# Masks put into the score banks a segment ahead, denominators behind the V products, LayerNorm steps behind the out-projection

## The chip, the cores and the metric

The kernel runs on one core of a Trainium2 chip. Five engines work beside each other, each through its own list of instructions in order: TensorE (PE, with its weight loads shown as PEld), VectorE (DVE), ScalarE (ACT), GpSimd (POOL) and SyncE (SP, which here only starts transfers). They wait for each other by semaphores. TensorE writes into PSUM, eight banks of 128 partitions by 2 KB; VectorE and ScalarE read PSUM and write the large memory SBUF. The metric is the device time of one execution in microseconds.

## The reference

The reference computes a forward pass and all its gradients. The change concerns the forward pass of the first block, a transformer with a recurrent memory of 8 rows that goes through the sequence in 64 segments of 32 rows:

```python
n_seg = S // seg_len                      # 2048 // 32 = 64
mask = (idx[:, None] < M) | (idx[:, None] >= idx[None, :])
mem = mem0
for s in range(n_seg):
    xs = x[:, s * seg_len:(s + 1) * seg_len, :].copy()
    h = jnp.concatenate([mem, xs], axis=1)            # 8 + 32 rows of 512
    q = jnp.einsum('btd,dhe->bhte', h, Wq)            # 32 heads of 128; k, v alike
    scores = jnp.einsum('bhqe,bhke->bhqk', q, k) * scale
    scores = jnp.where(mask[None, None], scores, -1000000000.0)
    p = _softmax(scores, axis=-1)
    o = jnp.einsum('bhqk,bhke->bhqe', p, v)
    o = jnp.einsum('bhte,hed->btd', o, Wo)
    mem = o[:, :M, :].copy()                          # goes into the next segment
    outs.append(o[:, M:, :])
```

x here is a LayerNorm of the input, scaled and shifted by a modulation. A gated MLP follows, and then the gradients by all inputs. Each segment needs the memory rows of the one before, so the 64 segments form one chain.

## The kernel before

The kernel has stages: `phase2` is the forward loop over the 64 segments, `phase3` the MLP, `phase4` and `phase5` the gradients. Only the forward loop and two helpers are touched. In the forward loop every engine's order is the order in which the Python code issues the instructions: a call at the end of the loop (`self.pin(i0)`) ties each instruction to the one before it on its engine. Waits between engines come from a framework that follows which tile, and which PSUM buffer, an instruction reads or writes.

Four segments make a tile of 128 rows; `s4` is the place of a segment in its tile. The 32 heads are held in 11 groups of three heads (a group is 120 rows wide: three heads of 40 rows, of which 8 are memory rows, 24 the first rows of the segment and 8 its last rows), and the 11 groups in three parts (`pi` = 0, 1, 2) of 4, 4 and 3 groups, one PSUM bank for each part.

A segment goes like this. The projections k, q and v multiply the segment's columns `hT` with the weights, in halves (`col_pass`, L249), and DVE and ACT cast each half to rows `RA`. The halves of k and q are turned (`turns`, L258) and copied into the columns `kT` and `qT`. Then:

- `st_exp(pi)` (L686 to L694): for each group of a part a score product and behind it a mask product, which adds the mask by an identity; then ACT's exp of the whole part into `ET`.
- `vshift` (L719 to L726), between the second and the third part: three products shift the rows of the last V heads in a bank (`sh_ps`), and DVE copies that bank into `Vst`.
- `den(pi)` (L698 to L704): sums over the keys, one column for each group, in a bank of their own (`dc_ps`). `recip` (L709) takes their reciprocals to `rden` on DVE.
- `pv(pi)` (L728 to L733): the V products, into `or_ps`.
- `ost(pi)`: `or_ps` times `rden` into `Ost`; parts 0 and 2 by DVE (L745), part 1 by four instructions of ACT (L742).
- `ott(pi)`: `Ost` is transposed (L716) and copied into `OT`, parts 0 and 2 by DVE, part 1 by ACT.
- `outproj` (L752, products at L220): the out-projection, 64 products into `at_ps`. `split_pair` splits it into a high part (ACT, L227) and a low part (DVE, L229), and `sum_pair` (L232) folds both by products (L237) into `at_ft`, whose memory rows ACT copies into the next segment's `hT` (L842).

Into this chain other work is set at fixed places: `fill(s4, ...)` projects and turns, for the next tile, the last 8 rows of each segment, which do not depend on the memory (slots f1, f2 and turn; POOL's tail copies, L65, put them into `kT` and `qT`); `TailRows` projects the outputs of those rows, once a tile, in two pieces; `pop_later` does the transposes that store a segment's output (L330); for s = 8 to 23 `mod_rest` computes parts of the modulation; and `p1` computes the LayerNorm of a tile two tiles ahead, in five steps: 0 loads, 1 takes statistics, 2 scales (L401, L402), 3 shifts and stores (L406, L407), 4 transposes (L412). Step 0 is at the start of s4 = 0; steps 1 to 3 stand between the k and the q projection of s4 = 1 to 3; step 4 stands before `ott(0)` at s4 = 3.

PSUM is divided into seven buffers that all these tiles share, and one for `TailRows`.

Of the kernel before, what the change touches and what calls it, by code (L numbers as in the profile page):

```python
# [40 lines left out]
class K:  # L41
# [389 lines left out]
    def phase2(self):  # L431
# [13 lines left out]
        with ExitStack() as ctx:  # L445
            wp = ctx.enter_context(tc.tile_pool(name="p2w", bufs=1))
            Wo = wp.tile([128, H, D], BF16, name="Wo")
            maskT = wp.tile([128, 120], BF16, name="maskT128")
# [51 lines left out]
            with tc.tile_pool(name="p0", bufs=1) as p0:  # L500
# [7 lines left out]
                nc.tensor.matmul(m_ps[:], lhsT=perm[:], rhs=mcol[:], start=True, stop=True)  # L508
                nc.vector.tensor_copy(maskT[0:120, :], m_ps[:])
                p1(0, 0)  # L510
# [88 lines left out]
            def b_pieces(t):  # L599
# [10 lines left out]
                def turn_b(x):  # L610
                    bt[x] = btp.tile([128, 8, 128], BF16, name="b_cols" + x)
                    tps = [turn_half(RBt[x], hf) for hf in range(2)]

                    def f():
                        for hf in range(2):
                            self.evac(("act", "dve")[hf], bt[x][:, 4 * hf:4 * hf + 4, :], tps[hf][:])

                    evacs.append(f)
# [23 lines left out]
            mod_r = []  # L642
            tail = TailRows(self, sb2, psp, psb, 1, "ao", self.AOB, 2)

# [10 lines left out]

            i0 = len(self.traced())
            for s in range(NS):
                s4 = s % nseg_t
# [27 lines left out]
                def st_exp(pi):  # L686
                    st_ps = ps_f32("st_ps")
                    for j in range(min(PG, G - pi * PG)):
                        g = pi * PG + j
                        nc.tensor.matmul(st_ps[:, j, 0:120], lhsT=x120(KT, g), rhs=QT[:, g * 120:g * 120 + 120],  # L690
                                         start=True, stop=False)
                        nc.tensor.matmul(st_ps[:, j, 0:120], lhsT=self.ident[:, :], rhs=maskT[:, :], start=False, stop=True)
                    n = min(PG, G - pi * PG)
                    nc.scalar.activation(part3(ET, pi)[:, 0:n, 0:120], st_ps[:, 0:n, 0:120], AF.Exp, scale=cfg.scale)  # L694

                den_ps = [None]

                def den(pi):  # L698
                    if pi == 0:
                        den_ps[0] = psp.tile([128, G], F32, name="dc_ps", tag="p")  # L700
                    n = min(PG, G - pi * PG)
                    for j in range(n):
                        g = pi * PG + j
                        nc.tensor.matmul(den_ps[0][:, g:g + 1], lhsT=ET[:, g * GW:(g + 1) * GW], rhs=self.ones[:, 0:1],  # L704
                                         start=True, stop=True)

                def recip(a, b):
                    a, b = a * PG, min(b * PG, G)
                    nc.vector.reciprocal(rden[:, a:b], den_ps[0][0:120, a:b])  # L709

# [8 lines left out]
                def vshift():  # L719
                    sh = ps_f32("sh_ps")  # L720
                    shf = sh[:].rearrange("p g x -> p (g x)")
                    for hl in range(3):
                        nc.tensor.matmul(shf[32 * hl:32 * hl + 32, 0:384], lhsT=self.ident[96:128, 96:128],
                                         rhs=RA["v"][96:128, 384 * hl:384 * hl + 384], start=True, stop=True,
                                         tile_position=(96, 32 * hl))
                    nc.vector.tensor_copy(Vst[0:96, 1024:1408], shf[0:96, 0:384])  # L726

                def pv(pi):  # L728
# [62 lines left out]
                st_exp(1)  # L791
                vshift()
# [39 lines left out]
                if s + 1 < NS:  # L832
                    tails_in("kq", s + 1)
# [1042 lines left out]
class TailRows:  # L1876

    def __init__(self, k, pool, psp, psb, n, name, dram_b, npieces=4, tags=""):  # L1880
        self.k, self.pool, self.psp, self.psb, self.n, self.name = k, pool, psp, psb, n, name
        self.dram_b, self.npieces, self.tags = dram_b, npieces, tags
        self.cur = None
        self.pieces = []
        self.whole = None
# [10 lines left out]
    def begin(self, s0, ws):  # L1896
# [8 lines left out]
        def piece(u):  # L1905
            def f():
                if u == 0:
                    st["ps"] = self.psb.tile([128, 512], F32, name=f"{self.name}_tps", tag="b")
# [118 lines left out]
```

## Time and profile before

| what | value |
|---|---|
| median of 6 runs | 3183.32 us (3179.41 to 3192.8) |
| profiled execution | 3192.96 us, span 3191.1 us, mean granted clock 0.983 |
| busy over the span | PE 2980.8, PEld 1728.6, DVE 1588.4, ACT 1159.7, POOL 1475.8 us |
| forward loop, 50 to 1010 us | PE 926.65, PEld 598.05, DVE 595.52, ACT 468.75, POOL 626.99 us busy of 960 |
| transfers in that stretch | DMA engines busy 0.84, 203 GB/s |

A line of the timeline gives the start in us from the beginning of the span, the length (of several equal instructions together where it ends in x and a number), the engine, the line of the kernel, the operation, what it writes and reads, the sizes, and in brackets how long the engine had been idle before it and whose work ended that. TensorE's products are pipelined: a row of 0.22 us does not keep the next from starting 0.05 us later, so busy time on PE also counts products that are only draining. A line on a tile gives the shortest, median and longest duration in ns.

### The profile page before, as it was taken

Reading aid. Unit: us, or ns where it says so; the run is one execution under the profiler, and the core shown is the slowest. Engines: PE = TensorE matmul, PEld = TensorE weight load, DVE = VectorE, ACT = ScalarE, POOL = GpSimd, SP = SyncE. Lnnn points to the kernel's source line nnn. Section 1 sums busy time; section 2 is a strip of 40 time slices with the busy share of each in tenths; the row PEclk is TensorE's granted clock in tenths of the full one; section 3 lists DMA queues with packets and bytes.
Section 4 is the critical chain, followed back from the end, with each engine's and each line's share of the span. In section 5 each row is a group of like instructions: output and inputs, shape, how many; then the busy total and the mean of one; then the engine's idle time right before and its main releaser. Section 6 shows DMA issues by size and latency. Waiting matters only on the chain.

```text
span 3191.1 us, 98793 instructions
## 1 busy us (share of the span) xinstructions
PE 2980.8 (93%) x39993; PEld 1728.6 (54%) x40069; DVE 1588.4 (50%) x3770; ACT 1159.7 (36%) x2829; POOL 1475.8 (46%) x2973
## 2 busy tenths in 40 slices
PE   5999999999998899989999999999999969999999
PEld 3666666666665444445555555555555534445454
DVE  4666666665655777642255444555545521332221
ACT  2454444444444333322244444444444410010011
POOL 3666666666664566521244444444444421232322
PEclk8999999999999899999999999999999989999999
DMA  9788888788888799897599999999999999998885
GB/s 300 199 213 202 203 204 203 204 201 212 198 200 244 175 221 215 218 281 242 176 262 256 255 245 257 263 266 259 274 267 258 258 224 227 226 218 190 205 228 154
DMA packets 958892, 726.12 MB, mean 228 GB/s; under 512 B 656018, under 2 KB 831138, under 8 KB 958308
## 3 DMA queue, kind: packets, MB, share of 16 engines
q1 hardware_dynamic: 827940, 508.77, 70.7%
q0 software_dynamic: 59056, 148.62, 13.8%
q10 hardware_dynamic: 71440, 62.40, 7.8%
q8 instruction: 316, 5.18, 0.7%
q14 instruction: 140, 1.15, 0.1%
HBM read 294.91 MB, written 276.33 MB: 179 GB/s over the span
## 4 chain that ended last, share of the span: by engine, by line
PE 30%; DMA 11%; issue 10%; POOL 3%; ACT 2%; DVE 1%; SPq 1%; ACTq 0%; POOLq 0%; DVEq 0%
PE dh_ps L212 9%; PE pass_ps L249 4%; PE g_ps L1509 3%; PE gps L1820 3%; PE dh_tps L212 2%; DMA rows<-OSR 2%; DMA rows<-DKR 2%; PE tps L1424 2%; DMA dOst<-RBd 1%; PE dp_ps L1488 1%; PE dp_ps L1496 1%; ACT RAd L61 1%; DMA rows<-DQR 1%; DMA out_dram<-ot 1%; DMA Kst<-KST 1%
## 5 line engine op out<-in xcount | busy, mean ns | idle before, releaser
L1820 PE MATMUL gps<-rows,hrows 128*128 128x512 bf16 (+2 forms) x2124 | 417.4, 356 | 6.7 <-DVE ot L63 2.8
L1820 PEld LDWEIGHTS <-hrows 128*128 128x128 bf16 x2160 | 211.8, 98 | 210.7 <-issue 7.4
L249 PEld LDWEIGHTS <-hT 128*32 128x32 bf16 x6144 | 158.0, 97 | 161.2 <-issue 1.6
L1538 POOL COPY dOst<-RAd 96x512 bf16<-96x512 bf16 x128 | 78.1, 610 | 355.8 <-DVE RAd L63 345.2
L852 POOL TENSOR_TENSOR Pst<-Pst,rden 120x1408 bf16<-120x1408 bf16 x63 | 160.4, 2546 | 111.7 <-issue 77.8
L1824 POOL DMA_DIRECT2D out_dram<-ot x108 | 81.3, 753 | 238.1 <-DVE ot L63 140.2
L63 DVE CAST ot<-gps 128x512 bf16<-128x512 f32 (+3 forms) x76 | 47.9, 632 | 254.8 <-PE gps L1820 133.1
L309 DVE TENSOR_TENSOR dh_lo<-dh_ps,dh_hi 128x256 bf16<-128x256 f32 x128 | 48.4, 420 | 241.5 <-ACT dh_hi L305 241.5
L1833 PE MATMUL gps5o<-WoT,rows 128*128 128x512 bf16 x588 | 132.4, 384 | 25.2 <-DMA rows<-OSR 24.4
L61 ACT ACTIVATE ot<-gps 128x512 bf16<-128x512 f32 (+3 forms) x75 | 41.1, 548 | 288.0 <-PE gps L1820 138.6
L212 PE MATMUL dh_ps<-WvT,dVT 128*32 128x512 bf16 x2048 | 135.0, 381 | 0.0
L1498 DVE SCALAR_TENSOR_TENSOR dS<-dp_ps,Pst_l 128x512 bf16<-128x512 f32 (+1 forms) x192 | 112.2, 640 | 42.5 <-PE dp_ps L1496 42.4
L249 PE MATMUL pass_ps<-Wv,hT 128*32 128x512 bf16 x2048 | 133.3, 380 | 0.0
L249 PE MATMUL pass_ps<-WoT,dyT 128*32 128x512 bf16 x2048 | 121.9, 380 | 5.2 <-ACT dyT L1597 5.2
L220 PE MATMUL at_ps<-Wo,OT 128*32 128x256 bf16 x4096 | 124.3, 274 | 0.5 <-DVE OT L63 0.2
L61 ACT ACTIVATE dVT<-g_ps 128x512 bf16<-128x512 f32 (+1 forms) x192 | 107.8, 562 | 45.3 <-PE g_ps L1509 27.1
L249 PE MATMUL pass_ps<-Wk,hT 128*32 128x512 bf16 x2048 | 122.7, 382 | 1.5 <-ACT hT L842 1.1
L212 PE MATMUL dh_ps<-WkT,dKT 128*32 128x512 bf16 x2048 | 122.9, 380 | 0.1
L212 PE MATMUL dh_ps<-WqT,dQT 128*32 128x512 bf16 x2048 | 122.4, 379 | 0.0
L249 PE MATMUL pass_ps<-Wq,hT 128*32 128x512 bf16 x2048 | 121.6, 379 | 0.0
L63 DVE CAST RA0v<-pass_ps 128x512 bf16<-128x512 f32 x128 | 88.3, 690 | 65.3 <-PE pass_ps L249 65.1
L694 ACT ACTIVATE ET<-st_ps 128x480 bf16<-128x480 f32 (+1 forms) x192 | 96.0, 535 | 54.2 <-ACT qT L61 37.3
(411 smaller groups left out, 7032.7 us busy)
## 6 DMA issues: line engine op xcount, KB each, us to landing
OSR<-Ost SPq DMA_DIRECT2D x64, 352.0 KB
OT<-OT SPq DMA_DIRECT2D x64, 352.0 KB
VT<-VTr SPq DMA_DIRECT2D x64, 352.0 KB
PS<-Pst SPq DMA_DIRECT2D x64, 352.0 KB
OT_l<-OT SPq DMA_DIRECT2D x64, 352.0 KB
Pst_l<-PS SPq DMA_DIRECT2D x64, 352.0 KB
VT_l<-VT SPq DMA_DIRECT2D x64, 352.0 KB
DKR<-rows_x POOLq DMA_DIRECT2D x64, 352.0 KB, 5.7
```

The costliest lines, as they stand in the source:

```text
L61: return nc.scalar.activation(out, in_, AF.Copy)
L63: return nc.vector.tensor_copy(out, in_)
L212: self.nc.tensor.matmul(ps[32 * j:32 * j + 32, :], lhsT=lhsT, rhs=w, start=(n < 4), stop=(n >= total - 4), tile_position=(0, 32 * j))
L220: nc.tensor.matmul(ps[32 * j:32 * j + 32, :], lhsT=x[k], rhs=w[k][:, 256 * d:256 * d + 256], start=(n == 0), stop=(n == total - 1), tile_p ...
L249: self.nc.tensor.matmul(ps[32 * j:32 * j + 32, :], lhsT=lhs(c), rhs=rhs, start=(c == 0), stop=(c == DC - 1), tile_position=(0, 32 * j))
L694: nc.scalar.activation(part3(ET, pi)[:, 0:n, 0:120], st_ps[:, 0:n, 0:120], AF.Exp, scale=cfg.scale)
L852: nc.gpsimd.tensor_tensor(Pst[0:120, :, :], Pst[0:120, :, :], rden[:, :].unsqueeze(2).to_broadcast([120, G, 128]), op=ALU.mult)
L1498: nc.vector.scalar_tensor_tensor(out=part3(dS, pi), in0=ps[:, 0:n, :], scalar=cfg.scale, in1=part3(Pst, pi), op0=ALU.mult, op1=ALU.mult)
L1509: nc.tensor.matmul(ps[:, j, :], lhsT=lh[:, g * GW:(g + 1) * GW], rhs=rh[:, g * GW:(g + 1) * GW], start=True, stop=True)
L1820: nc.tensor.matmul(ps[:, 0:ng * E], lhsT=hrows[:, tp_, c * 128:(c + 1) * 128], rhs=rows[:, tp_, 0:ng * E], start=(tp_ == 0), stop=(tp_ == ...
L1824: nc.gpsimd.dma_start(outw[c * 128:(c + 1) * 128, h0:h0 + 3 * (ng - 1) + 1:3, :], ot[:, 0:ng * E].rearrange("p (h e) -> p h e", e=E))
L1833: nc.tensor.matmul(pss[gg][:], lhsT=rows[:, tp_, gg * E:(gg + 1) * E], rhs=dyrows[:, tp_, :], start=(tp_ == order[0]), stop=(tp_ == order[ ...
```

## The change

Each of the three score banks is now reserved (a pool `pst` of three banks) and gets its mask by one product over all its groups, `mask_mm`, a segment ahead; the score products add to it. `mask_mm` is called three times before the loop, and in each segment: two times before `ott(0)` where no turn stands there, else one time behind `ott(0)` and one behind `ott(1)`; the last behind `ott(2)`.

The denominators stand behind the V products of their part, and have no bank of their own: parts 0 and 1 are written into columns of the `vshift` bank that the shift does not use, part 2 into free columns of the third `or_ps`. `ott` copies parts 0 and 2 by ACT and part 1 by DVE. `sum_pair` takes all high products first, then the low ones. `turn_b` uses one bank for both halves. The LayerNorm steps 1 to 3 stand behind the out-projection of s4 = 0 to 2, before the tail copies and `split_pair`. The shared buffers are five, and `TailRows` takes its bank from them.

```diff
-        for c in range(self.cfg.DC):
-            for i in range(2):
+        for i in range(2):
+            for c in range(self.cfg.DC):
                 self.nc.tensor.matmul(ft[:, c, :], lhsT=parts[i][:, (c % 2) * 128:(c % 2) * 128 + 128],
-                                      rhs=self.foldhalf[:, c // 2, :], start=(i == 0), stop=(i == 1))
+                                      rhs=self.foldhalf[:, c // 2, :], start=(i == 0 and c == 0), stop=(i == 1),
+                                      skip_group_check=True)
...
-            psp = ctx.enter_context(tc.tile_pool(name="p2ps", bufs=7, space=PSUM))
-            psb = ctx.enter_context(tc.tile_pool(name="p2psb", bufs=1, space=PSUM))
+            psp = ctx.enter_context(tc.tile_pool(name="p2ps", bufs=5, space=PSUM))
+            pst = ctx.enter_context(tc.tile_pool(name="p2pst", bufs=3, space=PSUM))
...
+            def mask_mm(pi):
+
+                n = min(PG, G - pi * PG)
+                ps = masked[pi] = pst.tile([128, PG, GW], F32, name="st_ps", tag="st")
+                nc.tensor.matmul(ps[:, 0:n, 0:120], lhsT=self.ident[:, :], rhs=maskT[:, 0:n, :], start=True, stop=False,
+                                 skip_group_check=True)
...
                 def st_exp(pi):
-                    st_ps = ps_f32("st_ps")
-                    for j in range(min(PG, G - pi * PG)):
-                        g = pi * PG + j
-                        nc.tensor.matmul(st_ps[:, j, 0:120], lhsT=x120(KT, g), rhs=QT[:, g * 120:g * 120 + 120],
-                                         start=True, stop=False)
-                        nc.tensor.matmul(st_ps[:, j, 0:120], lhsT=self.ident[:, :], rhs=maskT[:, :], start=False, stop=True)
+                    st_ps = masked.pop(pi)
...
-                        nc.tensor.matmul(den_ps[0][:, g:g + 1], lhsT=ET[:, g * GW:(g + 1) * GW], rhs=self.ones[:, 0:1],
+                        nc.tensor.matmul(st_ps[:, j, 0:120], lhsT=x120(KT, g), rhs=QT[:, g * 120:g * 120 + 120],
+                                         start=False, stop=True, skip_group_check=True)
...
+                def den(pi, ps):
+                    for g in range(pi * PG, min(pi * PG + PG, G)):
+                        nc.tensor.matmul(ps[:, PG - 1, g:g + 1], lhsT=ET[:, g * GW:(g + 1) * GW], rhs=self.ones[:, 0:1],
                                          start=True, stop=True)
...
-                    self.evac("act" if pi == 1 else "dve", part3(OT, pi)[:, 0:n, :], ps)
+                    self.evac("dve" if pi == 1 else "act", part3(OT, pi)[:, 0:n, :], ps)
...
-                if 1 <= s4 <= 3:
-                    p1(s // nseg_t + P1_AHEAD, s4)
                 proj("q", 0, "dve")
...
-                den(0)
                 or0 = pv(0)
+                den(0, sh)
...
-                den(1)
-                recip(0, 2)
                 or1 = pv(1)
+                den(1, sh)
+                recip(0, 2, sh)
                 ost(0, or0, "dve")
                 ost(1, or1, "act")
-                den(2)
                 or2 = pv(2)
-                recip(2, 3)
+                den(2, or2)
+                recip(2, 3, or2)
                 ost(2, or2, "dve")
+                more = list(range(NP)) if s + 1 < NS else []
+                turned = bool(slots.get((s4, "turn")))
                 fill(s4, "turn")
                 if s4 == 3:
                     p1(s // nseg_t + P1_AHEAD, 4)
+                    turned = True
+                if more and not turned:
+                    mask_mm(more.pop(0))
+                    mask_mm(more.pop(0))
                 ott(0)
+                if len(more) > 1:
+                    mask_mm(more.pop(0))
                 ott(1)
+                if len(more) > 1:
+                    mask_mm(more.pop(0))
                 ott(2)
+                if more:
+                    mask_mm(more.pop(0))
...
                 at_ps = outproj()
                 evac_turned()
+                if s4 < 3:
+                    p1(s // nseg_t + P1_AHEAD, s4 + 1)
```

More of the change, by code (lines that the diff above doesn't have):

```diff
@@ L447, in phase2 @@
             Wo = wp.tile([128, H, D], BF16, name="Wo")
-            maskT = wp.tile([128, 120], BF16, name="maskT128")
+            maskT = wp.tile([128, PG, 120], BF16, name="maskT128")
             nc.vector.memset(maskT[:], NEG)
@@ L508, in phase2 @@
                 nc.tensor.matmul(m_ps[:], lhsT=perm[:], rhs=mcol[:], start=True, stop=True)
[L509 removed]
+                nc.vector.tensor_copy(maskT[0:120, :, :], m_ps[:].unsqueeze(1).to_broadcast([120, PG, 120]))
                 p1(0, 0)
@@ L611, in turn_b @@
                     bt[x] = btp.tile([128, 8, 128], BF16, name="b_cols" + x)
-                    tps = [turn_half(RBt[x], hf) for hf in range(2)]
+                    tp = psp.tile([128, 8, 128], BF16, name="turn_ps", tag="p")
+                    for i in range(8):
+                        nc.tensor.transpose(tp[:, i, :], RBt[x][:, i * 128:(i + 1) * 128], self.ident[:, :])
                     def f():
                         for hf in range(2):
-                            self.evac(("act", "dve")[hf], bt[x][:, 4 * hf:4 * hf + 4, :], tps[hf][:])
+                            self.evac(("act", "dve")[hf], bt[x][:, 4 * hf:4 * hf + 4, :], tp[:, 4 * hf:4 * hf + 4, :])
                     evacs.append(f)
@@ L642, in phase2 @@
             mod_r = []
-            tail = TailRows(self, sb2, psp, psb, 1, "ao", self.AOB, 2)
+            tail = TailRows(self, sb2, psp, psp, 1, "ao", self.AOB, 2, ptag="p")
+            masked = {}
+            def mask_mm(pi):
[3 more added lines that the diff above has]
+                                 skip_group_check=True)
             def tails_in(xs, s):
@@ L656, in phase2 @@
             i0 = len(self.traced())
+            for pi in range(NP):
+                mask_mm(pi)
             for s in range(NS):
@@ L686, in st_exp @@
                 def st_exp(pi):
-                    st_ps = ps_f32("st_ps")
-                    for j in range(min(PG, G - pi * PG)):
-                        g = pi * PG + j
-                        nc.tensor.matmul(st_ps[:, j, 0:120], lhsT=x120(KT, g), rhs=QT[:, g * 120:g * 120 + 120],
-                                         start=True, stop=False)
-                        nc.tensor.matmul(st_ps[:, j, 0:120], lhsT=self.ident[:, :], rhs=maskT[:, :], start=False, stop=True)
[L693 to L700, printed above, removed]
+                    st_ps = masked.pop(pi)
                     n = min(PG, G - pi * PG)
@@ L703, in den, with recip @@
                         g = pi * PG + j
-                        nc.tensor.matmul(den_ps[0][:, g:g + 1], lhsT=ET[:, g * GW:(g + 1) * GW], rhs=self.ones[:, 0:1],
+                        nc.tensor.matmul(st_ps[:, j, 0:120], lhsT=x120(KT, g), rhs=QT[:, g * 120:g * 120 + 120],
+                                         start=False, stop=True, skip_group_check=True)
+                    nc.scalar.activation(part3(ET, pi)[:, 0:n, 0:120], st_ps[:, 0:n, 0:120], AF.Exp, scale=cfg.scale)
+                def den(pi, ps):
+                    for g in range(pi * PG, min(pi * PG + PG, G)):
+                        nc.tensor.matmul(ps[:, PG - 1, g:g + 1], lhsT=ET[:, g * GW:(g + 1) * GW], rhs=self.ones[:, 0:1],
                                          start=True, stop=True)
-                def recip(a, b):
+                def recip(a, b, ps):
                     a, b = a * PG, min(b * PG, G)
-                    nc.vector.reciprocal(rden[:, a:b], den_ps[0][0:120, a:b])
+                    nc.vector.reciprocal(rden[:, a:b], ps[0:120, PG - 1, a:b])
                 def transposes_part(src, pi, w=GW):
@@ L726, in vshift @@
                     nc.vector.tensor_copy(Vst[0:96, 1024:1408], shf[0:96, 0:384])
+                    return sh
                 def pv(pi):
@@ L791, in phase2 @@
                 st_exp(1)
-                vshift()
+                sh = vshift()
                 st_exp(2)
@@ L1876, with __init__ @@
 class TailRows:
-    def __init__(self, k, pool, psp, psb, n, name, dram_b, npieces=4, tags=""):
+    def __init__(self, k, pool, psp, psb, n, name, dram_b, npieces=4, tags="", ptag="b"):
         self.k, self.pool, self.psp, self.psb, self.n, self.name = k, pool, psp, psb, n, name
-        self.dram_b, self.npieces, self.tags = dram_b, npieces, tags
+        self.dram_b, self.npieces, self.tags, self.ptag = dram_b, npieces, tags, ptag
         self.cur = None
@@ L1907, in f @@
                 if u == 0:
-                    st["ps"] = self.psb.tile([128, 512], F32, name=f"{self.name}_tps", tag="b")
+                    st["ps"] = self.psb.tile([128, 512], F32, name=f"{self.name}_tps", tag=self.ptag)
                 for n in range(u * per, (u + 1) * per):
```

## The prediction

> **What bounds the kernel now.** I read four views in this order: the engine table and slices of the page, the busy time of the forward stretch, the timeline of one of its segments engine by engine, and the groups of the tiles that the change moves.
>
> ```profile
> PE 2980.8 (93%) x39993; PEld 1728.6 (54%) x40069; DVE 1588.4 (50%) x3770; ACT 1159.7 (36%) x2829; POOL 1475.8 (46%) x2973
> ...
> 50.00:1010.00 960.00, 926.65 (x17786) 598.05 (x17784) 595.52 (x1479) 468.75 (x1275) 626.99 (x1339) 1.00 0.84 203
> ```
>
> The change lies in the forward loop, the first 1010 us, where PE reads 926.65 of 960 us busy at a granted clock of 1.00. That looks like an engine with nothing to win but instructions. The timeline says otherwise. Segment 33 of the 64, from its first score product at 559.81:
>
> ```profile
> 559.81 0.23 PE L690 MATMUL st_ps<-qT,kT 128*128 128x120 bf16 x1
> ...
> 560.75 0.34 PE L723 MATMUL sh_ps<-RA0v,ident 32*32 32x384 bf16 x3
> 561.35 0.24 PE L704 MATMUL dc_ps<-ones,ET 128*128 128x1 bf16 x4
> 561.45 0.38 PE L733 MATMUL or_ps<-Vst,ET 128*128 128x128 bf16 x4
> 561.67 0.24 PE L704 MATMUL dc_ps<-ones,ET 128*128 128x1 bf16 x4
> 561.77 0.38 PE L733 MATMUL or_ps<-Vst,ET 128*128 128x128 bf16 x4
> 562.21 0.21 PE L704 MATMUL dc_ps<-ones,ET 128*128 128x1 bf16 x3
> 562.32 0.33 PE L733 MATMUL or_ps<-Vst,ET 128*128 128x128 bf16 x3
> 562.94 1.09 PE L716 MATMUL tps<-ident,Ost 128*128 128x128 bf16 x11 [0.29 <-DVE Ost L745]
> 563.87 0.22 PE L330 MATMUL ao_b_tp<-ident,ao_b_tb 128*128 128x128 bf16 x1
> 563.93 0.22 PE L330 MATMUL at_tp<-ident,at_tb 128*128 128x128 bf16 x1
> 564.08 0.40 PE L220 MATMUL at_ps<-Wo,OT 128*32 128x256 bf16 x6
> ```
>
> ```profile
> 560.00 0.69 DVE L63 CAST RA0v<-pass_ps 128x512 bf16<-128x512 f32 x1 [0.31 <-PE pass_ps L249]
> 561.14 0.55 DVE L726 CAST Vst<-sh_ps 96x384 bf16<-96x384 f32 x1 [0.45 <-PE sh_ps L723]
> 561.95 0.21 DVE L709 RECIPROCAL rden<-dc_ps 120x8 f32<-120x8 f32 x1 [0.26 <-PE dc_ps L704]
> 562.19 0.69 DVE L745 TENSOR_TENSOR Ost<-or_ps,rden 120x512 bf16<-120x512 f32 x1
> 562.80 0.17 DVE L709 RECIPROCAL rden<-dc_ps 120x3 f32<-120x3 f32 x1
> 563.08 0.56 DVE L745 TENSOR_TENSOR Ost<-or_ps,rden 120x384 bf16<-120x384 f32 x1
> 563.55 0.88 DVE L63 COPY OT<-tps 128x512 bf16<-128x512 bf16 x2
> ```
>
> From the first score product to the out-projection is 4.27 us here, and the chain is DVE's from 561.95 on: reciprocal, first Ost, second reciprocal, second Ost (ends 563.64), the last transposes behind it, then two small transposes and the projection. PE waits between 562.54 and 562.94 for the first Ost. So a segment's length follows the time of the first reciprocal, 2.14 us after the first score. By place in the tile (s4 = 0, 1, 2, 3) the projection starts 4.41, 4.27, 4.21 and 4.31 us after the first score, nearly the same in every segment; what follows it, up to the next first score, is 10.48 us wherever nothing interferes.
>
> **Part 1: masks.** Removed: 11 mask products at the score products' pitch of 0.052 us, 0.58 us of PE. Added: three products of 480, 480 and 360 columns; no row shows one. At the pitch of the 120-column rows they cost 0.21, 0.21 and 0.16 us, again 0.58; at the worst each stands for the whole 0.39 us of a 512-column pass product. I take the pitch, since four of those pass products, side by side, follow each other every 0.22 us; the other end would add 64 x 0.23 = 15 us for the last mask. Work is moved, not saved. The first exp starts when four scores are done: four fewer products, 0.21 us earlier. But the vshift products (L723) wait for the second RA0v cast (560.69; they start 0.06 later, 560.75), and that does not move: the third score part, behind them, and so the third exp, gains only 0.16 us. Where the masks go: in s4 0 and 1 two stand in the 0.40 us (soon longer) wait before the first transposes, free while that wait exists (without it 0.42 us). The third stands behind the last transposes, which come at the end of DVE's chain, so its 0.16 us lies on the path everywhere. In s4 2 and 3 the masks stand between the transposes.
>
> **Part 2: denominators.** They no longer have a bank; the first two parts write the spare columns of the vshift bank, and in the program the first of them waits for DVE's copy out of that bank (L726). That copy ends at 561.69, so the denominators cannot start before 561.75; before, the first four ran at 561.35, beside the copy. Behind them in PE's order stand the second V products (0.22 us) and the second denominators: 561.75 + 0.10 + 0.22 = 562.07, results 0.24 later, and DVE takes them up 0.04 later (as 561.67 + 0.24 to 561.95): the reciprocal at 562.35 instead of 561.95, **0.40 us late**, though exp was earlier. The wait for the first reciprocal by the third denominators (562.21) is gone; the third part is not late, since DVE reaches its reciprocal only when the first Ost is done. In the 16 segments with modulation products the same order holds and the same 0.40.
>
> **Part 3: which engine copies OT.** OT parts 0 and 2 go to ACT, part 1 to DVE. ACT's four Ost pieces end at 563.47, so 563.87 when late by 0.40; its 0.60 us copy of part 0 then ends about 564.4, before PE gets to the projection, except in s4 3: there ACT has the 0.60 us copy hx (L414, whose next copy starts 0.50 later) in front.
>
> **Sum of parts 1 to 3 per segment.** s4 0 and 1: 0.40 + 0.16 s4 0 and 1: 0.395 + 0.158 = 0.55.. s4 2: the second mask also pushes the last transposes, past their input, by 0.10: 0.64. s4 3: ACT's pieces end 4.06 after the first score, hx starts 0.12 before that, part 0 starts 0.50 later and ends at 5.04, projection at 5.10 instead of 4.31: 0.79. Last tile, no turns: 0.55 for all. 34 x 0.55 + 15 x 0.64 + 15 x 0.79 = **+40 us**.
>
> **Part 4: fold sum.** Four hi products now stand before the lo products, which wait for at_lo 0.21 us after the first hi. Three products at 0.025 us leave the path: 64 x 0.08 = **-5 us**; the copy into hT behind them is covered by the next tile's 1 us of projection (the fill in slot f2), as before.
>
> **Part 5: LayerNorm steps.** Now they stand between the k and q casts on DVE:
>
> ```profile
> L401 DVE TENSOR_SCALAR xh<-x,mv,rstd x14: 540/2318/2869, 80.0 to 870.1; 128x512 f32<-128x512 bf16 x14
> ...
> 573.59 0.62 PE L258 MATMUL turn_ps<-ident,RA0q 128*128 128x128 bf16 x8 [0.39 <-DVE RA0q L63]
> ...
> 566.53 0.42 DVE L229 TENSOR_TENSOR at_lo<-at_ps,at_hi 128x256 bf16<-128x256 f32 x1 [1.84 <-ACT at_hi L227]
> ```
>
> L401 takes 0.54 us alone, 2.3 mostly: it lies beside POOL's L852 (569.39 for 2.54). The q turns wait. Against 7.38 us from fold sum to next score, the segments after s4 1 lost 8.0 us in total and those after s4 2 1.9: **-10 us** if all goes. The new place is DVE's 1.84 us wait before at_lo, for 0.54 + 0.69 us of scaling, or 0.68 of stats (plus two small ones), or 0.68 of shift. POOL's rstd and the H1ROWS issue (0.58) move ahead of its tail copies, which the scores need some 8 us later: nothing. SP's loads keep their place; x is loaded 17 us before its statistics. PSUM falls from seven general buffers to five; with the program's banks each reuse waits for something already past, v1 the nearest (the v0 cast ends 0.06 us before v1 starts): zero, at most 0.05 x 64 = 3.
>
> Sum: 40 - 5 - 10 = +25 us. The profiled execution took 3192.96 (span 3191.1), so 3218 for such a one; it stands 9.6 above the median, and the difference is carried to the median: 3183.3 + 25 = **3208**.
>
> **The rivals.**
> A: *the wait on the copy does not decide*. Then the first V products follow the third scores at once: 560.75 + 0.27 (vshift) + 0.16 = 561.18, V 0.22, denominators 0.10, V 0.22, denominators 0.24, 0.04: the reciprocal at 562.00, 0.05 late instead of 0.40. Per segment 0.35 us less, 64 x 0.35 = 22: +3, 3186. Against it: the copy's end, 1.88 us after the first score in nearly every segment.
> B, *faster: PE's work is the bound*, as 97% busy says. Then the exps' 0.21 us lead carries through, masks fill PE's waits, and the projection starts 0.21 earlier: 64 x 0.21 = 13, with 5 and 10: -28, 3155. It decides if the first reciprocal starts less than 2.14 us after the first score. Against it the idle before L716. The Trainium skill (Trainium Kernel Development and Optimization, Reading a trace) calls matmul busy time a bad metric because matmuls are pipelined, and would judge by weight loads; here they are busy 598 of 960 us, which agrees with the timeline.
> C, *slower still: the steps of part 5 collide at the new place* with POOL's tail copies (L65, 565.96 to 567.4): at L401's long 2.3 + 0.69 us, the end is past at_lo by about 1.1 us in s4 1, 14 x 1.1 = 15: 40 - 5 - 10 + 15 = +40, 3223. For it: L401's rows. Against: the partner then was one 2.54 us instruction, the tail copies are 0.19 to 0.36 us each. The Trainium skill (SBUF — State Buffer, SBUF: two separate sides) has VectorE and GpSimd share a port pair held exclusively for a whole instruction. That speaks for C; by its length rule the wait ends with one short copy, which speaks against the full price. No run here shows the place yet.
>
> **How the numbers follow.** Forecast 0.62 (+15 to +33, 3198 to 3216), A 0.14, B 0.10, C 0.14. A splits: about half within 0.2% (6.4 us), which is about what a measurement tells from no change; the rest is mostly slower. Slower 0.62 + 0.14 + 0.06 = 0.82, same 0.08, faster 0.10. The range takes in most of A and C, and part of the dearer mask, and leaves out B: 3184 to 3227.
>
> **What would show it.** Right: in the profile after, the first denominators start 0.06 us after the Vst copy ends; the first reciprocal is 2.54 us after the first score (2.14 now); the projection starts at about 4.96, 4.82, 4.85, 5.10; the first exp starts 0.21 us nearer the first score; the scaling line (L401 before) falls to 0.5 to 0.9 us and no turn waits for RA0q; segments near 15.3 us against 14.75. Wrong: a reciprocal at 2.2 or earlier (A, B), or at_lo waiting for xh (C).

## The result, and the profile after

| | median of its runs | beside it |
|---|---|---|
| before | 3184.89 us | 3174.27 to 3200.37, 47 runs |
| after | 3198.08 us | 3187.88 to 3207.57, 23 runs |
| ratio | 1.0041 | 95% interval 1.003 to 1.0051 |

The changed kernel is slower by 13 us (10 to 16), the sign that was forecast and inside the range; it lies at the lower end of the likeliest case's own 3198 to 3216, and the 3208 us themselves are 10 too many. Its profiled execution took 3201.98 us, span 3200.0, mean granted clock 0.986.

The engine table of the page of the kernel after:

```profile
PE 2985.7 (93%) x39481; PEld 1702.1 (53%) x39557; DVE 1533.1 (48%) x3706; ACT 1188.9 (37%) x2893; POOL 1475.1 (46%) x2973
```

The busy times of the kernel after in the forward stretch (window and length, then PE, PEld, DVE, ACT, POOL, the clock, the DMA share and GB/s):

```profile
50.00:1010.00 960.00, 919.45 (x17005) 566.49 (x17002) 535.19 (x1391) 488.21 (x1313) 614.15 (x1316) 1.00 0.76 200
```

The kernel after holds 512 PE products fewer, yet its loop is longer, and in the same 960 us every engine but ACT is busy for less time. Such a table tells that something waits, not what. The timeline of segment 33 does; here is PE from the first score product at 568.71 on, in the kernel after:

```profile
568.71 0.59 PE L705 MATMUL st_ps<-qT,kT 128*128 128x120 bf16 x8
569.23 0.74 PE L730 MATMUL sh_ps<-RA0v,ident 32*32 32x384 bf16 x3
569.91 0.33 PE L705 MATMUL st_ps<-qT,kT 128*128 128x120 bf16 x3
570.08 0.39 PE L741 MATMUL or_ps<-Vst,ET 128*128 128x128 bf16 x4
570.62 0.24 PE L711 MATMUL sh_ps<-ones,ET 128*128 128x1 bf16 x4 [0.16 <-DVE Vst L733]
570.72 0.38 PE L741 MATMUL or_ps<-Vst,ET 128*128 128x128 bf16 x4
570.94 0.24 PE L711 MATMUL sh_ps<-ones,ET 128*128 128x1 bf16 x4
...
571.29 0.56 PE L654 MATMUL st_ps<-maskT,ident 128*128 128x480 bf16 x2
572.21 1.02 PE L723 MATMUL tps<-ident,Ost 128*128 128x128 bf16 x11 [0.36 <-DVE Ost L753]
573.07 0.32 PE L654 MATMUL st_ps<-maskT,ident 128*128 128x360 bf16 x1
...
573.43 0.73 PE L220 MATMUL at_ps<-Wo,OT 128*32 128x256 bf16 x20
```

And DVE in the same segment of the kernel after:

```profile
570.01 0.55 DVE L733 CAST Vst<-sh_ps 96x384 bf16<-96x384 f32 x1 [0.42 <-PE sh_ps L730]
571.22 0.21 DVE L716 RECIPROCAL rden<-sh_ps 120x8 f32<-120x8 f32 x1 [0.65 <-PE sh_ps L711]
571.46 0.69 DVE L753 TENSOR_TENSOR Ost<-or_ps,rden 120x512 bf16<-120x512 f32 x1
572.07 0.17 DVE L716 RECIPROCAL rden<-or_ps 120x3 f32<-120x3 f32 x1
572.28 0.56 DVE L753 TENSOR_TENSOR Ost<-or_ps,rden 120x384 bf16<-120x384 f32 x1
```

Follow the bank `sh_ps`. DVE's copy out of it ends at 570.56; the first denominators, which write it, start at 570.62, though the V products ahead of them were under way at 570.08 and the exp of part 0 had been done for longer still. The second V products and denominators stand behind. So DVE, idle for 0.65 us, gets its first reciprocal at 571.22, 2.51 us after the first score, where it was 2.14.

The medians by place in the tile, in us after the first score of a segment (before, then after; the first and the last segment are left out):

| | s4 0 | s4 1 | s4 2 | s4 3 |
|---|---|---|---|---|
| first exp | 0.63, 0.42 | 0.68, 0.47 | 0.68, 0.47 | 0.68, 0.47 |
| Vst copy ends | 1.88, 1.86 | 1.88, 1.86 | 1.88, 1.86 | 1.88, 1.86 |
| first reciprocal | 2.14, 2.51 | 2.14, 2.51 | 2.14, 2.51 | 2.14, 2.51 |
| second Ost of DVE ends | 3.83, 4.13 | 3.83, 4.12 | 3.83, 4.13 | 3.83, 4.13 |
| out-projection starts | 4.41, 4.87 | 4.27, 4.72 | 4.21, 4.84 | 4.31, 4.97 |
| next first score | 14.89, 15.28 | 15.58, 15.13 | 14.99, 15.25 | 14.79, 15.38 |

In the last row, segments of the kernel before that LayerNorm steps or modulation products held up raise the medians at s4 1 and 2; undisturbed ones take 14.75 and 14.70 there. In the 16 segments that are held up by modulation products (9 to 24, counted from 0) the first reciprocal comes at 2.80 before, in one of them at 3.14, and at 3.15 after: 0.35 late where it was 2.80.

The 62 segments between the first and the last took 936.8 us before and 953.8 after: +17.0. Between the last out-projection of the loop and the first product of the MLP there were 38.8 us before and 34.4 after: -4.4. Together +12.6, near the +13.2 of the medians; but the two profiled executions differ by only 9.0 us. What lies outside the 62 segments took between 2231 and 2254 us in the profiled executions of all kernels here, so the experiments are read by the time of these segments first, and by the time of the whole second.

### The profile page after: what moved, and what is told of

It reads as the page before. It is cut to its first block, busy times and chain, and to the rows that moved or that the text cites. A ratio compares the mean times of both kernels' runs of the same rounds, so it can differ in the third digit from the quotient of the medians.

```text
span 3200.0 us, 97713 instructions
## 1 busy us (share of the span) xinstructions
PE 2985.7 (93%) x39481; PEld 1702.1 (53%) x39557; DVE 1533.1 (48%) x3706; ACT 1188.9 (37%) x2893; POOL 1475.1 (46%) x2973
## 4 chain that ended last, share of the span: by engine, by line
PE 36%; issue 9%; DMA 6%; ACT 2%; POOL 2%; DVE 1%; SPq 1%; ACTq 0%; POOLq 0%; DVEq 0%
PE dh_ps L212 10%; PE gps L1840 5%; PE pass_ps L250 4%; PE gps5o L1853 4%; PE g_ps L1529 3%; PE dh_tps L212 2%; DMA rows<-DKR 2%; DMA Kst<-KST 2%; PE tps L1444 2%; PE dp_ps L1508 1%; ACT RAd L61 1%; PE dp_ps L1516 1%; PE dh_ft L319 1%; DMA rows_x<-dVT 1%; PE turn_ps L1410 1%
## 5 line engine op out<-in xcount | busy, mean ns | idle before, releaser
L63 DVE CAST dKT<-g_ps 128x512 bf16<-128x512 f32 (+1 forms) x192 | 112.2, 640 | 1.3
```

Of the source, the lines that this page charges most:

```text
L63: return nc.vector.tensor_copy(out, in_)
```

## The experiments

Two theories stood against each other. **The bank**: the 0.37 us come from the denominators sharing a bank that DVE still reads. **The order**: they come from the denominators standing behind the V products, so that DVE gets the sums later, whatever bank they are in. A third, that the masks behind the transposes are the main cost, is tried further down. Each kernel below is the changed kernel with one edit unless it says otherwise; "loop" is the time of the same 62 segments in its profiled execution.

### The bank alone

All denominators go into spare columns of the third V bank (`or2`), their order is kept:

```diff
+                or2 = ps_f32("or_ps")
                 or0 = pv(0)
-                den(0, sh)
+                den(0, or2)
...
                 or1 = pv(1)
-                den(1, sh)
-                recip(0, 2, sh)
+                den(1, or2)
+                recip(0, 2, or2)
...
-                or2 = pv(2)
+                pv(2, or2)
```

> The changed kernel, with the denominators of all parts in the spare columns of the third or_ps bank instead of the vshift bank; their order behind the V products is kept. Theory 1 (the copy out of the vshift bank holds the denominators): they start as soon as the first V products are issued, the first reciprocal goes from 2.51 to about 2.19 us after the first score, each segment loses 0.32 us, 64 x 0.32 = 20 us: about 3178, 0.994 of the changed kernel and 0.998 of the kernel before. Theory 2 (standing behind the V products is what costs): the reciprocal stays within 0.05 us of 2.51, about 3195 to 3198. Theory 3 (the mask products behind the transposes are the cost): no change, 3198.

Measured: 3181.68 us, 0.9993 of before (0.9978 to 1.0009); loop 934.6, so 19.2 less than after, 0.31 a segment. The first reciprocal is at 2.19. PE and, below it, DVE in segment 33 of this kernel, whose first score is at 558.64:

```profile
560.01 0.39 PE L741 MATMUL or_ps<-Vst,ET 128*128 128x128 bf16 x4
560.24 0.24 PE L711 MATMUL or_ps<-ones,ET 128*128 128x1 bf16 x4
560.34 0.38 PE L741 MATMUL or_ps<-Vst,ET 128*128 128x128 bf16 x4
560.56 0.24 PE L711 MATMUL or_ps<-ones,ET 128*128 128x1 bf16 x4
561.10 0.33 PE L741 MATMUL or_ps<-Vst,ET 128*128 128x128 bf16 x3 [0.30 <-DVE rden L716]
```

```profile
559.95 0.55 DVE L733 CAST Vst<-sh_ps 96x384 bf16<-96x384 f32 x1 [0.42 <-PE sh_ps L730]
560.84 0.21 DVE L716 RECIPROCAL rden<-or_ps 120x8 f32<-120x8 f32 x1 [0.34 <-PE or_ps L711]
```

The first denominators now run at 560.24, in the middle of the copy (559.95 to 560.50), while the copy and the first V products stand where they stood. The new wait, 0.30 us of the third V products for the first reciprocal, because they now share its bank, costs nothing: DVE needs them only after its first Ost. The bank theory holds: the shared bank is 0.32 of the 0.37 us. It is not the whole price of parts 1 to 3, though. The loop is shorter than before (934.6 against 936.8) only because the LayerNorm and fold parts are in it too; the kernel before with those two alone, shown below, has 922.5.

### The order alone, and both

Here is the edit of the order in the shared bank; the second kernel has the same order with `or2` for the bank:

```diff
+                den(0, sh)
                 or0 = pv(0)
-                den(0, sh)
...
-                or1 = pv(1)
                 den(1, sh)
                 recip(0, 2, sh)
+                or1 = pv(1)
```

> The changed kernel, with the denominators of parts 0 and 1 put ahead of the V products of their part again, but left in the vshift bank. Theory 1 (the bank): they wait for the same copy, the V products of part 0 now wait behind them, and the first reciprocal stays at 2.51 us after the first score: 3198, within 3 us. Theory 2 (the order): the reciprocal comes 0.22 us earlier, the length of four V products, 64 x 0.22 = 14 us: 3184. Theory 3 (masks): 3198.

> The changed kernel, with both: all denominators in the third or_ps bank, and ahead of the V products of their part. Theory 1: the first denominators start behind the third scores, at 1.37 us, the second behind four V products at 1.69, and the reciprocal at 1.97 us after the first score, 0.54 earlier than in the changed kernel and 0.17 earlier than before the change: 64 x 0.54 = 35 us, about 3163, 0.993 of the kernel before. Theory 2 (order alone): 3184. Theory 3 (masks): 3198.

With the old order in the shared bank: 3212.76 us, 1.0075 (1.0047 to 1.0102), loop 962.9; the reciprocal is at 2.63, not at the 2.51 expected. With both: 3165.45 us, 0.9939 (0.9916 to 0.9962), loop 921.8, reciprocal at 1.97. PE of the first of these, then of the second, both in segment 33 (first scores at 572.83 and 551.25):

```profile
574.03 0.33 PE L705 MATMUL st_ps<-qT,kT 128*128 128x120 bf16 x3
574.74 0.24 PE L711 MATMUL sh_ps<-ones,ET 128*128 128x1 bf16 x4 [0.38 <-DVE Vst L733]
574.96 0.38 PE L741 MATMUL or_ps<-Vst,ET 128*128 128x128 bf16 x4
575.18 0.24 PE L711 MATMUL sh_ps<-ones,ET 128*128 128x1 bf16 x4
```

```profile
552.45 0.33 PE L705 MATMUL st_ps<-qT,kT 128*128 128x120 bf16 x3
552.62 0.24 PE L711 MATMUL or_ps<-ones,ET 128*128 128x1 bf16 x4
552.72 0.38 PE L741 MATMUL or_ps<-Vst,ET 128*128 128x128 bf16 x4
552.94 0.24 PE L711 MATMUL or_ps<-ones,ET 128*128 128x1 bf16 x4
```

The first of these was profiled in the shortest of its six executions (3196.12 us); its loop is the longer one all the same. So the order has a sign of its own in each bank. In the shared bank, denominators in front hold up the V products too: four small products wait 0.38 us, and the V products behind them start 0.22 after them where they follow after 0.10 in the other kernel; that is the 0.12 by which 2.51 was missed. V products first are right there, worth 9.1 us of loop. In the third V bank, denominators first are right, worth 12.8. With bank and order both mended the loop (921.8) is back at the 922.5 of the LayerNorm and fold parts alone: together they make up for the price of parts 1 to 3.

### Where the masks go

```diff
-                if more and not turned:
-                    mask_mm(more.pop(0))
+                while more:
                     mask_mm(more.pop(0))
                 ott(0)
-                if len(more) > 1:
-                    mask_mm(more.pop(0))
                 ott(1)
...
```

> The changed kernel, with all three mask products of a segment ahead of the first transposes, none between or behind them. Theory 1 (the masks are the smaller part): the projection then waits for ACT's copy of OT part 0, at about 4.65 us after the first score: 0.15 us less at s4 0, 0.07 at s4 1, 0.19 at s4 2, nothing at s4 3 where ACT has the hx copy in front; 6 us in all, 3192. Theory 3 (the masks behind the transposes are the main cost): 0.16 us or more in every segment and 0.26 at s4 2 and 3, 10 to 14 us, 3184 to 3188. Theory 2: 3192 as theory 1.

Measured: 3191.92 us, 1.0017 (1.0 to 1.0035); loop 948.3, 5.5 less than after. The out-projection starts at 4.71, 4.64, 4.70 and 4.97. All three masks in PE's wait ahead of the first transposes save 0.16, 0.08 and 0.14 us; at s4 3 nothing, since PE waits there for ACT's copy of OT (0.27 us in that kernel). So the masks are a smaller cost beside the bank.

### Who copies OT

```diff
-                    self.evac("dve" if pi == 1 else "act", part3(OT, pi)[:, 0:n, :], ps)
+                    self.evac("act" if pi == 1 else "dve", part3(OT, pi)[:, 0:n, :], ps)
```

> The changed kernel, with OT parts 0 and 2 copied by DVE and part 1 by ACT, as before the change. If ACT's copy of part 0 sets the projection only at s4 3 (4.97 us after the first score, behind hx), it starts 0.13 us earlier there and nowhere else: 15 x 0.13 = 2 us, 3196. Rival (the copies on ACT hold the projection everywhere): 0.2 us in every segment, 13 us, 3185.

Measured: 3195.11 us, 1.0034 (1.0012 to 1.0056); loop 952.4, 1.4 less. The out-projection starts 0.08 earlier at s4 3 (4.89) and within 0.01 elsewhere. The time differs from after by no more than its interval; the term is 0.08 us in one segment of four.

### The LayerNorm steps

First the move by itself, in the kernel before:

```diff
-                if 1 <= s4 <= 3:
-                    p1(s // nseg_t + P1_AHEAD, s4)
                 proj("q", 0, "dve")
...
                 at_ps = outproj()
+                if s4 < 3:
+                    p1(s // nseg_t + P1_AHEAD, s4 + 1)
```

> The kernel before, with only the LayerNorm steps moved behind the out-projection. If the steps cost 10 us where they were and fit into DVE's 1.84 us wait at the new place: 3175, 0.997 of the kernel before. Rival (collision with POOL's tail copies at the new place): at_lo waits for xh in some segments and the time is 3185 or more.

Measured: 3174.96 us, 0.9971 (0.9952 to 0.9991); loop 926.4, so -10.4. Then the opposite: the steps put back between k and q in the changed kernel.

> The changed kernel, with the LayerNorm steps 1 to 3 put back between the k and q projections. If the move took DVE's scaling out of the way of the q casts, the long L401-like rows (2.3 us beside POOL's 2.54) and the waits of the q turns come back: 10 us slower than the changed kernel, 3208. Rival (the move gains nothing, since the segments are longer now and DVE has more room): no difference, 3198.

Measured: 3198.38 us, 1.0049 (1.0027 to 1.0071), as the changed kernel itself; loop 954.7, so only +0.9. The same move is worth 10 us in one kernel and 1 in the other. The scaling's rows, in the kernel before and then with the steps put back, each with POOL's product `Pst` that lies beside it (segment 33; POOL's timeline line, then DVE's):

```profile
569.39 2.54 POOL L852 TENSOR_TENSOR Pst<-Pst,rden 120x1408 bf16<-120x1408 bf16 x1 [1.40 <-issue]
...
569.86 2.35 DVE L401 TENSOR_SCALAR xh<-x,mv,rstd 128x512 f32<-128x512 bf16 x1
```

```profile
576.70 2.53 POOL L872 TENSOR_TENSOR Pst<-Pst,rden 120x1408 bf16<-120x1408 bf16 x1
...
578.72 0.79 DVE L402 TENSOR_SCALAR xh<-x,mv,rstd 128x512 f32<-128x512 bf16 x1
```

In both the scaling ends 0.28 us after POOL's product ends: 572.21 and 571.93 in the one, 579.51 and 579.23 in the other. It does so in 12 of 14 tiles before and in all 14 with the steps put back. What differs is where the product starts: 0.3 to 0.7 us ahead of the scaling in seven of the 14 tiles before, 2.0 us ahead in eight of the 14 with the steps put back. The price of the place is what is left of POOL's product, and the change had moved that product by other means: in this segment POOL starts it right behind its tail copies, without the 1.40 us of waiting. (What POOL waited for in the kernel before the trace doesn't name, and this was not followed further.)

That reading asks for a trial: put the steps back and make the product late again. Two scratch products on POOL ahead of it do that, and the same two in the changed kernel, its steps where the change put them, are the control.

```diff
+            scr = sb2.tile([128, 384], BF16, name="scr", bufs=1)
+            self.nc.gpsimd.memset(scr[:], 0.0)
...
                 def norm(s=s, Pst=Pst, rden=rden):
+                    for _ in range(2):
+                        nc.gpsimd.tensor_tensor(scr[:], scr[:], scr[:], op=ALU.mult)
                     nc.gpsimd.tensor_tensor(Pst[0:120, :, :], Pst[0:120, :, :],
```

> The changed kernel with the LayerNorm steps back between the k and q casts (as in the kernel before) and with GpSimd's normalisation product (Pst, 2.53 us) made late by two scratch products of 384 elements ahead of it. Theory: what the old place costs is set by where the Pst product ends, since the scaling (L402) ended 0.28 us after it in the kernel before and with the steps back alike; with the steps back alone the product began 2.02 us ahead of the scaling, in the kernel before about 0.5 us ahead. The scratch products take some 0.7 us each by the Pst product's rate (2.53 us for 1408 elements), so the product begins about 0.6 us ahead, the scaling takes 2.2 us in place of 0.8, and the segments after s4 1 lose some 0.6 us each, 14 of them, as before: loop sum near 963 us in place of 954.7, time near 3207. Rival: the loss in the kernel before came from something that the other parts of the change removed; then the scaling may grow but nothing waits for it, and the loop sum stays at 955, time 3198.

> The changed kernel as it is, with the same two scratch products ahead of GpSimd's Pst product: the control. Both theories: the LayerNorm steps stand elsewhere and GpSimd's next work waits 2.5 us a segment for RA0v, so a product 1.4 us later is covered; loop sum 954, time 3198. If GpSimd's lateness costs anything by itself it shows here, up to 64 x 0.2 = 13 us.

Measured: 3207.91 us, 1.0074 (1.0053 to 1.0095), loop 963.1 with the steps back; 3198.32 us, 1.0031 (1.0016 to 1.0046), loop 953.7 in the control. Both came out as the theory had it. The rows of the scaling, steps put back, then with the late product, then in the control:

```profile
L402 DVE TENSOR_SCALAR xh<-x,mv,rstd x16: 547/798/1789, 5.9 to 884.4; 128x512 f32<-128x512 bf16 x16
```

```profile
L402 DVE TENSOR_SCALAR xh<-x,mv,rstd x16: 545/2487/2512, 5.9 to 892.8; 128x512 f32<-128x512 bf16 x16
```

```profile
L402 DVE TENSOR_SCALAR xh<-x,mv,rstd x16: 536/539/596, 5.8 to 878.5; 128x512 f32<-128x512 bf16 x16
```

The lateness alone costs nothing; the lateness and the old place together cost 8.4 us of loop over the steps put back, and the segments at s4 1 lose 0.74 us each at the median.

### The fold sum

The kernel before with the LayerNorm move and the fold sum's new order:

```diff
-        for c in range(self.cfg.DC):
-            for i in range(2):
+        for i in range(2):
+            for c in range(self.cfg.DC):
```

> The kernel before with two parts of the change alone: the LayerNorm steps behind the out-projection, and the fold sum with its four hi products ahead of the lo ones. Parts add: the fold takes 0.30 us in place of 0.38, so the loop sum falls from 926.4 (LayerNorm move alone) by 64 x 0.08 = 5 to 921.3, time near 3170, 0.9956 of before. If the lo products' wait for at_lo sets the end of the fold, the gain is nothing: 3175.

Measured: 3170.34 us, 0.9943 (0.9917 to 0.9968); loop 922.5 against 926.4. From its first product to its last the fold takes 0.30 us where it took 0.38, as in the changed kernel.

### The parts that gain, put together

From these: denominators in the third V bank and first, DVE copying OT 0 and 2, mask 0 behind the second V products, mask 1 behind the third ones or, where a turn stands there, between the transposes of parts 0 and 1, and mask 2 inside the fold sum, in its wait for the low half.

```diff
         for i in range(2):
+            if i == 1 and between is not None:
+                between()
             for c in range(self.cfg.DC):
...
+                den(0, or2)
                 or0 = pv(0)
...
                 or1 = pv(1)
+                if s + 1 < NS:
+                    mask_mm(0)
...
-                more = list(range(NP)) if s + 1 < NS else []
+                more = [1] if s + 1 < NS else []
...
-                ft = self.sum_pair(psp, parts, "at", "p")
+                ft = self.sum_pair(psp, parts, "at", "p", (lambda: mask_mm(2)) if s + 1 < NS else None)
```

> Both undone that cost: the denominators in the third or_ps bank and ahead of the V products (as in e3_bank_order); the first mask product behind the second V products, where PE waits for the reciprocal, the second ahead of the first transposes or, where a turn stands there, behind them, the third between the high and low products of the fold, where PE waits for at_lo; OT copied by the engines of the kernel before. If masks behind the last transposes cost 0.16 us a segment and the rest is as in e3_bank_order: 0.11 us less at s4 0 and 1, 0.23 at s4 2, 0.27 at s4 3, 11 us: about 3154, 0.990 of the kernel before. Rival (the masks were free already): 3165, as e3_bank_order.

Measured: 3153.3 us, 0.9914 of before (0.9897 to 0.993), faster than the kernel before and the changed one; loop 910.4, 26.4 less than before. PE in its segment 33, first score at 545.93:

```profile
547.73 0.38 PE L743 MATMUL or_ps<-Vst,ET 128*128 128x128 bf16 x4
547.95 0.37 PE L656 MATMUL st_ps<-maskT,ident 128*128 128x480 bf16 x1
548.16 0.21 PE L713 MATMUL or_ps<-ones,ET 128*128 128x1 bf16 x3
548.27 0.33 PE L743 MATMUL or_ps<-Vst,ET 128*128 128x128 bf16 x3
548.44 0.36 PE L656 MATMUL st_ps<-maskT,ident 128*128 128x480 bf16 x1
548.89 1.02 PE L725 MATMUL tps<-ident,Ost 128*128 128x128 bf16 x11
549.75 0.22 PE L333 MATMUL ao_b_tp<-ident,ao_b_tb 128*128 128x128 bf16 x1
```

The wide masks stand where PE would wait anyway, and behind the last transposes there is no product of theirs any more. The out-projection starts at 4.17, 4.02, 3.97 and 4.17 us after the first score; the mask inside the fold makes it 0.34 us instead of 0.30.

## Why the prediction was right, and where its sizes were off

**The bank (part 2): right in mechanism and size.** The first denominators start 0.06 us after the copy ends, as written, and the reciprocal comes at 2.51 against 2.54 forecast; the copy itself ended 0.02 earlier. The kernel with the bank alone undone shows that 0.32 us of the lateness are this. The order would have cost 0.22 by itself (2.19 against 1.97 in the third V bank), most of it covered by the 0.17 us that PE is ahead after the scores (first denominators at 1.37 in the kernel with both, at 1.54 before). The wait itself is a semaphore wait of the program. The Trainium skill (PSUM — Partial Sum Buffer, Terms) counts a write by TensorE to a bank while VectorE reads it, in the same quadrant, as a collision, an error. No run here shows such a collision, since every kernel that shares the vshift bank waits for the copy; disjoint columns without the wait were not tried.

**Parts 1 to 3: too dear by a sixth.** The loop shows +17.0, of which the LayerNorm move is -10.4 and the fold some -5 (62 x 0.08), so these parts come to +32 where the forecast's +40 over 64 segments makes 39 over 62. By the out-projection's own lateness, summed over the same segments, they come to +32 too. The term that was mis-sized is the 0.395 of "0.395 + 0.158": it takes all that the first reciprocal is late as lateness of what follows. The second Ost ends only 0.30 late, because it follows the second reciprocal after 0.21 us (572.07 to 572.28) where it was 0.28; why, the trace doesn't show. ACT's Ost pieces, too, end only 0.29 late, at 3.95 us after the first score and not at 4.06. At s4 3 that is nearly all of the difference between 4.97 and the 5.10 forecast: hx starts at 3.82 instead of 3.94, and ACT's next copy 0.48 behind it, as put down (0.50). The kernel with the old copying engines prices ACT's copies at 0.08 there. At s4 2 the sum came out, 0.62 for 0.64, by two errors that cancel: the second Ost is earlier than forecast, but PE's own work from the first Ost on (which is 0.37 late), the masks between the transposes included, sets the start. The mask behind the last transposes was right: 573.07 to the next product at 573.22 is 0.15, for 0.16; and the pitch taken for a 480-column mask, 0.21 with 0.39 as the other end, is what the rows of the last kernel show (547.95 to 548.16).

**vshift: a step half wrong, without a price.** I had all its products wait for the second RA0v cast. In the changed kernel the first of the three does not: it starts at 0.52 us instead of 0.94. The second and third wait for the cast (569.64, 0.05 after its end at 569.59), so the copy ends where it did. And the forecast read its times off one segment as "nearly the same in every segment"; in the 16 segments with modulation products the out-projection comes at 4.9 to 5.3 us in the kernel before.

**Fold and LayerNorm (parts 4 and 5): right.** The fold is 0.08 us shorter, and the loop 3.9 for the 5 forecast; the move gave -10.4 for -10 in the kernel before. But the sum treats part 5 as independent of the others, and it isn't: put back into the changed kernel it costs 1 us, because the other parts had already moved POOL's product. In the sum this changes nothing, since each order of adding the parts ends at the same place; read as a price tag for the move, the -10 holds only in the old kernel.

**Left out: the end of the loop.** 4.4 us less between the loop and the MLP. PE's order of the weight transposes differs there, and the last wait ahead of the first MLP product, for `hdT`, is 2.11 us where it was 6.50. Whether the change did this is not shown. In the other kernels the stretch takes from 33.4 to 38.5 us, and in the control with the late product, whose loop and median time are those of the changed kernel, it takes 38.1. So these 4.4 us may belong to that one execution.

**The rivals.** A, that the copy does not decide, needed a reciprocal at about 2.19: that is what the kernel with the denominators in the third V bank has. B, PE's work as the bound, needed it under 2.14: the kernel with bank and order both does this, at 1.97, and is faster; so the lead was real, and the shared bank and the new order together are what kept it from showing. C needed a long scaling at the new place; its rows read 0.54 us in the loop. In segment 33 DVE's two steps end at 575.01 and POOL's first tail copy starts at 575.10, behind its two DMA issues; the long product starts 3.3 us or more after the scaling starts. The Trainium skill's rule behind C (SBUF — State Buffer, SBUF: two separate sides), an exclusive port pair for the whole instruction, fits what the old place shows: the scaling ends 0.28 us after POOL's product, however much is left of it; who holds the pair where both start together is taken up below.

## What to carry to other kernels

Before putting two results in one PSUM bank, look at who still reads that bank when the second is written: here spare columns were free, but the program's wait goes by the buffer, and four one-column products waited for a copy whose data they did not touch. Taking instructions off an engine is worth what the next wait leaves of it: against the kernel with the LayerNorm and fold parts alone (loop 922.5), 512 products fewer came with 31 us more in the shared bank and the new order, with under 1 us less when bank and order were mended, and with 12 us less once the masks stood in PE's own waits and DVE copied OT again. Price a move between two engines by where the partner's instruction ends, and price it again after every other edit that shifts the partner.

## What the runs showed that I had not expected

A DVE scaling that overlaps POOL's product ends 0.28 us after the product's end, be its length then 0.79, 1.79, 2.35 or 2.87 us. POOL need not even be first by the trace: at 689.80 us of the kernel before the product starts 0.05 us behind the scaling, and the scaling still takes 2.87 us; at 809.55 it starts 0.16 us behind, the scaling takes its 0.54, and the product 2.78 instead of 2.54. And a stall can cost more than its length: with the denominators in front in the shared bank, the V products behind them start 0.12 us later than without the stall. It need not: in the changed kernel the same four denominators wait 0.16 us, and the V products behind them follow after 0.10. What makes the difference is not shown.
